# Start-up of a fused convolution and two-layer kernel: 64x64 tiles in the first units, x parts paired by tokens, and a moved plan of slots

## The chip, the cores and the metric

The kernel runs on one core of a Trainium2 chip. The metric is the device time of one execution in microseconds (us). Before the change the median of three runs is 680.96 us (680.73 to 681.37).

## What is computed

x has 8 sequences of 4096 tokens with 192 features each. A causal convolution over 7 tokens is taken, with softmax weights that are shared by the 24 features of one of 8 heads; its output goes through two matrices (192 x 2048 and 2048 x 192) with a leaky ReLU between them. Cut to what matters:

```python
w = softmax(weight)                                  # 8 heads x 7 taps
x_pad = concatenate([zeros((B, 6, D)), x], axis=1)
conv = einsum('hk,bskhg->bshg', w, windows_of(x_pad))  # each token and its 6 predecessors
h = conv.reshape(B * S, 192) @ w_in                  # w_in 192 x 2048
out = maximum(0.01 * h, h) @ w_out                   # w_out 2048 x 192
```

## The kernel before

**Tiling.** A block is 512 tokens of two sequences (e = 0 and 1), which take the two halves of the 128 partitions: `xt` holds x transposed, features on the partitions, in three chunks of 64 features (c = 0, 1, 2). There are 32 blocks. The first two are cut in halves of 256 tokens, so the list `groups` begins with groups 0 to 3 of 256 tokens (T = 256) and goes on with whole blocks from group 4 (T = 512).

**The work of one group.** The convolution of a group gives `yt`. `mm1` (L488) makes one unit of the first product: 3 chunks by 2 sequences, into a PSUM tile `ph` of two buffers; ACT applies the leaky ReLU and writes `g` (L515). A group of 256 tokens has 8 units, u = 0 to 7, a whole block has 16. A step j is two units. The second product is cut into slots. In groups 1 to 4 a slot is two matmuls for 128 tokens each (`mm2_row_slot`, L533; tile `po`), from group 5 on it works on whole blocks (`mm2_slot`, L568; tile `acc2`, shown as `acc` in the profile).

**Row slots.** 16 pieces of 128 tokens make 8 pairs of 32 slots. A pair has two rounds of 16 slots; in the second round the two row tiles of the array change banks, and its first matmuls wait for a "seal" (L545 to L549, `seal_round`, L555). The seal of pair p is the copy `evac_o(2p - 1)` (L631) of the odd piece of the pair before, made to wait for the last matmul of round one. That copy is on ACT. The odd copy also releases the output DMA of its pair, which stands in SP's queue.

**Who does the convolution.** For groups 0 and 1 chunks 0 and 2 are matmuls against diagonal matrices (`pe_conv_jobs`, L244; L259 in the profile), the others are chains of 7 instructions on DVE (`conv_jobs`, L209; L222 and L228). In the loop the jobs of group i+1 (`ahead`) are given to DVE while group i runs. In group 0 the diagonal matmuls for group 1 are put between the units in three portions, `CUTS` (L53): 6 steps after u = 1, 5 after u = 3, 3 after u = 5, each of 4 matmuls.

**How x gets there.** The first two blocks are loaded in four parts of 256 tokens, q = 0 to 3 (`load_first`, L137). Parts 1 and 2 come through POOL's queue as rows (`x_rows`), are transposed by TensorE (`transpose_first`, L162; part 1 inside unit 0 between chunks 1 and 2, part 2 after unit 6) and are copied from PSUM to `xt` by DVE (`evac_first`, L190). Part 3 and the later blocks are transposed by DMAs on SP's queue (L199, L114).

**Weights.** `w_in` comes in two halves n = 0, 1 of 1024 columns. Each is loaded for one half of the partitions and copied to the other by `spread_down` (L321) and `spread_up` (L324), mostly on DVE, with `near` and `far` for the two halves of its columns.

**Array tiles.** A matmul's tile of the array follows from its operands: the diagonal matmuls are 64x64, `mm1` in groups 0 to 4 uses weights of 128 columns (64x128), from group 5 on 64x64; the row slots are 64x128 and the transposes of `x_rows` 128x64.

**What sets the order.** Engines work in program order, and the order is written by hand: `plan` (L650) gives the slots of each step in groups 2, 3 and 4, `between` (L656) says in which steps some of them are put before the units of that step. DVE's queue in group i holds, step by step, the jobs of the next group's convolution.

Of the kernel before, what the change touches and what calls it, by code (L numbers as in the profile page):

```python
# [11 lines left out]
BF16 = mybir.dt.bfloat16  # L12
# [3 lines left out]
def kernel(  # L16
# [8 lines left out]
    nc = tc.nc  # L25
# [10 lines left out]
    CH = 64  # L36
    NCH = D // CH
    ST = 512
    SUB = ST // 128
    HT = ST // 2  # L40
    HS = SUB // 2
# [3 lines left out]
    NHALF = 2  # L45
# [4 lines left out]
    for k in range(K):  # L50
        SKEW += [(2, k), next(pair)]
    SKEW += [(1, 5), (0, 6), (1, 6)]
    CUTS = {1: (0, 6), 3: (6, 11), 5: (11, 14)}  # L53
    GB = 32
    NR = D // (2 * GB)

# [8 lines left out]
    psum_o = ctx.enter_context(tc.tile_pool(name="po", bufs=4, space=bass.MemoryType.PSUM))  # L65
# [70 lines left out]

    def load_first(q):  # L137
        rows = x[0:2, q * HT : (q + 1) * HT, :].rearrange("e (s p) d -> p e s d", s=HS)
        if q == 0:
            x_nat[q] = stage_pool.tile([128, 2, HS, D], FP32, name="x_nat")  # L140
            for s in range(HS):
                nc.sync.dma_start(out=x_nat[q][:, :, s], in_=rows[:, :, s])
        elif q in x_rows:
            for e in range(2):
                nc.gpsimd.dma_start(out=x_rows[q][:, e], in_=rows[:, e])  # L145
        else:
            for c in range(NCH):
                for e in range(2):
                    nc.gpsimd.dma_start(  # L149
                        out=x_half[q][:, c, :, e, :],  # L150
                        in_=rows[:, e, :, c * CH : (c + 1) * CH],
                    )
# [7 lines left out]
    ptr = {}  # L160

    def transpose_first(q, mid=None):  # L162
        if q:
            t = psum_o.tile([128, HS, NCH, 128], BF16, name="ptr", tag="po")
            for s, c in product(range(HS), range(NCH)):
                for e in range(2):
                    nc.tensor.transpose(  # L167
                        out=t[e * CH : (e + 1) * CH, s, c, :],
                        in_=x_rows[q][:, e, s, c * CH : (c + 1) * CH],
                        identity=ident,  # L170
                    )
            ptr[q] = [t[:, s] for s in range(HS)]
            return
        ts = [
            psum_o.tile([128, NCH, 128], FP32, name=f"ptr{s}", tag="po") for s in range(HS)
        ]
        for s, t in enumerate(ts):
            if s and mid is not None:
                mid()
            for c in range(NCH):  # L180
                nc.tensor.matmul(
                    out=t[:, c, :],
                    lhsT=x_half[q][:, c, s, :, :].rearrange("p e k -> p (e k)"),
                    rhs=ident,
                    start=True,
                    stop=True,
                )
        ptr[q] = ts

    def evac_first(q, *copies):  # L190
        dst = xt[0][:, :, HALO + q * HT : HALO + (q + 1) * HT]
        dst = dst.rearrange("p c (s k) -> p s c k", s=HS)
        for s, t in enumerate(ptr.pop(q)):
            for cs in (slice(0, 1), slice(1, NCH)) if q == 0 and s else (slice(0, NCH),):
                copies[s](out=dst[:, s, cs], in_=t[:, cs])

    def transpose_half(q):
# [82 lines left out]
    def run(*lists):  # L280
        for slots in zip_longest(*lists, fillvalue=()):
            for both in slots:
                for job in both:
                    job()
# [36 lines left out]
    def spread_down(n, copy=nc.vector.tensor_copy, cols=slice(0, WF)):  # L321
        copy(out=w_in[n][0:CH, 1, cols], in_=w_in[n][CH:128, 0, cols])  # L322

    def spread_up(n, slots=slice(0, 3, 2), cols=slice(0, WF)):  # L324
        to = slice(slots.start // 2 + 1, (slots.stop - 1) // 2 + 2)
        nc.vector.tensor_copy(out=w_in[n][CH:128, to, cols], in_=w_in[n][0:CH, slots, cols])  # L326
# [153 lines left out]
    NSW = 2 * NHALF  # L480
# [150 lines left out]
    def evac_o(n):  # L631
        b, e, s = subs[n]
        rp, st = divmod(b, NB)
        if n % 2 == 0 or n >= LAST:
            osb[n] = o_pool.tile([128, 2, D], FP32, name="o_sb")
        o_sb = osb[n if n >= LAST else n - n % 2]
        copy = nc.scalar.copy if b < NHALF else nc.vector.tensor_copy
        ins = copy(out=o_sb[:, n % 2, :], in_=po.pop(n))  # L638
        if n >= LAST:
            t0 = st * ST + s * 128  # L640
            nc.sync.dma_start(out=out_rows[2 * rp + e, t0 : t0 + 128, :], in_=o_sb[:, n % 2, :])
        elif n % 2 == 1:
# [7 lines left out]
    plan = {  # L650
        0: [0] * 4,
        NSW - 2: [16, 8, 8, 16],
        NSW - 1: [8, 8, 16, 16],
        NSW: [16, 8, 8, 16, 8, 8, 16, 16],
    }
    between = {(1, 0): (3, 5)}  # L656
    for i, js in ((NSW - 2, (2, 3)), (NSW - 1, (1, 2)), (NSW, (2, 3, 5, 6))):
        between.update({(i, j): (0, 4) for j in js})
    slot = 0

    def mm2_slots(i, n):
        nonlocal slot
# [7 lines left out]
    for i, grp in enumerate(groups):  # L670
        blk, t0, T = grp
        steps = T // 64
        if t0 == 0:
            g[blk] = g_pool.tile([128, NFC, 2, ST], BF16, name="g", tag="g")
        quota = plan.get(i, [16] * 4 if T == HT else [5, 5, 6, 5, 5, 6, 8, 8])
# [6 lines left out]
        for j in range(steps):  # L682
            early = between.get((i, j), (0, 0))
            for u in range(2 * j, 2 * j + 2):
                mm2_slots(i, early[u % 2])
                mm1(grp, u, 128 if i <= NSW else CH)
                if i == 0 and u == 0:
                    evac_first(1, nc.vector.tensor_copy, nc.vector.tensor_copy)
                    spread_up(0, slice(2, 3), far)
                    conv_1 = conv_jobs(groups[1], (1,))  # L690
                    run([conv_1[:3]])
                    spread_down(1)
                    spread_up(1, slice(0, 1), near)
                    spread_up(1, slice(2, 3))
                    run([conv_1[3:5]])
                    spread_up(1, slice(0, 1), far)
                    run([conv_1[5:]])
                    pe_0, evac_0 = pe_conv_jobs(groups[1], 0)
                    pe_2, evac_2 = pe_conv_jobs(groups[1], 2, cross=True)
                if i == 0 and u in CUTS:  # L700
                    cut = slice(*CUTS[u])
                    run(pe_0[cut], pe_2[cut])
                if i == 0 and u == 5:
                    evac_0(nc.vector.tensor_scalar_mul)
                    evac_2(nc.vector.tensor_scalar_mul, nc.vector.tensor_scalar_mul)
                if i == 0 and u == 6:
                    transpose_first(2)
                    evac_first(2, nc.vector.tensor_copy, nc.vector.tensor_copy)
            jobs = ahead[per * j : per * (j + 1)]
            if T == ST:  # L710

# [56 lines left out]
```

## Time and profile before

| | before |
|---|---|
| median of 3 runs | 680.96 us (680.73 to 681.37) |
| span of the profiled execution | 679.2 us |
| TensorE matmul (PE) | 674.9 us, 99%, 12442 matmuls |
| TensorE weight load (PEld) | 446.3 us, 66% |
| VectorE (DVE) | 481.2 us, 71% |
| ScalarE (ACT) | 517.6 us, 76% |
| GpSimd (POOL) | 147.4 us, 22% |
| DVE in 17.30 to 46.20 us | 10.46 of 10.50, 9.20 of 9.20, 9.15 of 9.20 us |
| POOL waiting for landed transposes | 405.6 us, 27 times |

A share is busy time over the span. PE's matmul times are pipelined and overlap, so a share of 99% says that the array always had a matmul in flight, not that it ran at its peak. In a timeline row the first number is the start, the second the length of the merged row, then engine, line, operation, tile written and tiles read, shapes and count; square brackets give the idle time in front and what ended it. In the chain of waits each row is a start, a length, an engine and a tile with its line; the chain is followed back from the last instruction. "64*128" is the tile of the array in rows and columns.

### The profile page before, as it was taken

To read this page: it belongs to the slowest core of one execution; us is meant where nothing else is said; L and a number is where in the kernel's file an instruction comes from. 1 tells how busy PE (TensorE), PEld (TensorE's weight loads), DVE (VectorE), ACT (ScalarE), POOL (GpSimd) and SP (SyncE) were. 2 spreads that over 40 slices of the span, in tenths; PEclk is the share of its full clock that TensorE was granted. 3 is DMA by queue.
4 is the path that set the end of the run, shared out by engine and by line. 5 is a ranking of instruction groups with operands and counts; after the bars stand their busy time and mean duration, and the time that the engine had idled before them with its cause. 6 is when DMAs were issued, how large, how long until landed. Compare 5 with 4: busy or idle time off the path is not lost.

```text
span 679.2 us, 27092 instructions
## 1 busy us (share of the span) xinstructions
PE 674.9 (99%) x12442; PEld 446.3 (66%) x12442; DVE 481.2 (71%) x816; ACT 517.6 (76%) x601; POOL 147.4 (22%) x208
## 2 busy tenths in 40 slices
PE   9999999999999999999999999999999999999998
PEld 6997666666666666666666666666666666666667
DVE  7989477866768766778667687667786676876612
ACT  7899877777787777777777777778777777777781
POOL 8455221122211222211222112222022220000000
PEclk9999999999999999999999999999999999999999
DMA  9999755655737656556556566567365573321123
GB/s 149 99 119 104 52 85 83 84 64 67 96 74 93 76 54 86 84 85 86 66 63 92 80 92 78 56 83 94 73 87 69 60 96 71 72 56 33 34 49 94
DMA packets 213970, 53.27 MB, mean 78 GB/s; under 512 B 209312, under 2 KB 213536, under 8 KB 213856
## 3 DMA queue, kind: packets, MB, share of 16 engines
q0 software_dynamic: 98832, 13.97, 30.3%
q1 hardware_dynamic: 115008, 37.57, 28.0%
q8 instruction: 97, 1.59, 0.9%
q14 instruction: 17, 0.14, 0.1%
q10 hardware_dynamic: 16, 0.00, 0.0%
HBM read 28.31 MB, written 25.17 MB: 79 GB/s over the span
## 4 chain that ended last, share of the span: by engine, by line
PE 98%; DVE 1%; ACT 0%; issue 0%; ACTq 0%
PE ph L507 49%; PE acc L588 44%; PE po L525 5%; PE acc L259 0%; DVE diag L420 0%; PE ptr L167 0%; ACT L366 0%; ACTq L288 0%; DVE w_in L322 0%; DVE yt L465 0%; DVE o_sb L638 0%; DVE x_half L155 0%; ACT w L372 0%; DVE w_in L326 0%; ACT junk L366 0%
## 5 line engine op out<-in xcount | busy, mean ns | idle before, releaser
L515 ACT ACTIVATE g<-ph 128x1024 bf16<-128x1024 f32 x512 | 496.6, 1021 | 139.8 <-PE ph L507 139.6
L228 DVE SCALAR_TENSOR_TENSOR yt<-xt,wk,yt 128x512 bf16<-128x512 bf16 (+1 forms) x582 | 380.1, 715 | 0.2
L507 PE MATMUL ph<-yt,w_in 64*64 64x512 bf16 (+2 forms) x6048 | 377.5, 369 | 0.3 <-DVE yt L465 0.3
L588 PE MATMUL acc<-g,w_out 64*64 64x512 bf16 x5568 | 339.9, 376 | 0.0
L507 PEld LDWEIGHTS <-w_in 64*64 64x64 bf16 (+1 forms) x6048 | 229.7, 131 | 103.4 <-issue 1.1
L588 PEld LDWEIGHTS <-w_out 64*64 64x64 bf16 x5568 | 178.2, 118 | 118.8
L96 POOL DMA_DIRECT2D x_bf<-in_x_dram x180 | 133.9, 774 | 407.6 <-DMA xt<-x_bf 405.6
L610 DVE STREAM_TRANSPOSE o_t<-acc 128x512 f32<-128x512 f32 x87 | 72.9, 875 | 182.2 <-PE acc L588 182.2
L525 PE MATMUL po<-w_out,g 64*128 64x192 bf16 (+1 forms) x640 | 36.8, 243 | 0.0
L525 PEld LDWEIGHTS <-g 64*128 64x128 bf16 (+1 forms) x640 | 32.6, 95 | 3.2 <-issue 0.4
L222 DVE TENSOR_SCALAR yt<-xt,wk 128x512 bf16<-128x512 bf16 (+1 forms) x97 | 28.8, 320 | 2.4 <-DMA xt<-x_bf 2.4
L598 ACT COPY junk<-junk 128x1 f32<-128x1 f32 x58 | 11.1, 191 | 4.1
L638 DVE COPY o_sb<-po 128x192 f32<-128x192 f32 x8 | 2.8, 356 | 6.8 <-PE po L525 3.9
L638 ACT COPY o_sb<-po 128x192 f32<-128x192 f32 x16 | 5.1, 323 | 0.3
L259 PE MATMUL acc<-xt,diag 64*64 64x256 bf16 x126 | 4.7, 272 | 0.1
L149 POOL DMA_DIRECT2D x_half<-in_x_dram x6 | 4.3, 732 | 0.9 <-DMA w_in<-in_moe_w_in_dram 0.9
L259 PEld LDWEIGHTS <-diag 64*64 64x64 bf16 x140 | 3.7, 106 | 1.0 <-issue 0.4
L360 PE MATMUL warm<-const-bfloat16-1.0 128*128 128x512 bf16 (+2 forms) x8 | 3.3, 577 | 0.8 <-PEq L752 0.8
L145 POOL DMA_DIRECT2D x_rows<-in_x_dram x4 | 2.9, 746 | 0.0
L316 POOL DMA_DIRECT2D w_in<-in_moe_w_in_dram x5 | 2.9, 593 | 0.0
L360 PEld LDWEIGHTS <-const-bfloat16-1.0 128*128 128x128 bf16 x10 | 1.2, 128 | 2.2 <-issue 2.2
L326 DVE COPY w_in<-w_in 64x512 bf16<-64x512 bf16 (+1 forms) x7 | 2.3, 337 | 0.2
(52 smaller groups left out, 25.9 us busy)
## 6 DMA issues: line engine op xcount, KB each, us to landing
out_dram<-o_t SPq DMA_DIRECT2D x112, 192.0 KB, 4.7
x_bf<-in_x_dram POOLq DMA_DIRECT2D x180, 64.0 KB, 3.1
out_dram<-o_sb SPq DMA_DIRECT2D x8, 192.0 KB, 2.8
xt<-x_bf SPq DMA_TRANSPOSE x90, 3.2
w_out<-in_moe_w_out_dram POOLq DMA_DIRECT2D x2, 384.0 KB, 8.3
out_dram<-o_t SPq DMA_DIRECT2D x8, 96.0 KB, 2.4
out_dram<-o_sb SPq DMA_DIRECT2D x8, 96.0 KB, 1.7
w_in<-in_moe_w_in_dram POOLq DMA_DIRECT2D x2, 256.0 KB, 5.5
```

The costliest lines, as they stand in the source:

```text
L96: ins = nc.gpsimd.dma_start(out=t[:, c, :, e, :], in_=src[2 * rp + e, :, :, c * CH : (c + 1) * CH],)
L222: lambda s=src, d=dst, c=c: nc.vector.tensor_scalar_mul(d, s, wk[:, c, 0:1])
L228: lambda s=src, d=dst, c=c, k=k: nc.vector.scalar_tensor_tensor(out=d, in0=s, scalar=wk[:, c, k : k + 1], in1=d, op0=mybir.AluOpType.mult, ...
L259: lambda k=k, p=p, a=a, ps=ps, to=to, acc=accs[e]: nc.tensor.matmul(out=acc[to, :T], lhsT=diag[c][ps, p, k, :], rhs=xt[0][ps, c, a : a + T ...
L360: nc.tensor.matmul(out=to[:, 0:cols], lhsT=ones[:, 0:128], rhs=ones[:, 0:cols], start=True, stop=True,)
L507: nc.tensor.matmul(out=ph[m : m + M, e, i * T : (i + 1) * T], lhsT=w_in_of(f, e, c, m, m + M), rhs=y[ps, c, t0 : t0 + T], start=(c == chun ...
L515: act = nc.scalar.activation(out=g[blk][:, nf * u : nf * (u + 1), :, t0 : t0 + T], in_=ph.rearrange("p e (i t) -> p i e t", i=nf), func=my ...
L525: return nc.tensor.matmul(out=po[m], lhsT=g[b][ps, fc, e, s * 128 : (s + 1) * 128], rhs=w_out[ps, fc, :], start=start, stop=stop,)
L588: ins = nc.tensor.matmul(out=acc2[gi, r][e * CH : (e + 1) * CH, 0:T], lhsT=w_out_of(ps, fc, r), rhs=g[b][ps, fc, e, t0 : t0 + T], start=fi ...
L598: seal = nc.scalar.copy(out=junk, in_=junk)
L610: nc.vector.transpose(out=osb[gi, 0][:, 0 : T // GB, :, r], in_=acc2.pop((gi, r))[:, 0:T].rearrange("p (j k) -> p j k", k=GB),)
L638: ins = copy(out=o_sb[:, n % 2, :], in_=po.pop(n))
```

## The change

Parts 1 and 2 of x are loaded with two neighbouring tokens on a partition, where before a partition held tokens p and p + 128. For part 1 the 12 transposes of 128x64 become 24 of 64x64 into two PSUM tiles, each with half of the tokens; both parts' copies to `xt` now take the tokens in pairs, and part 2's copies go by chunk (three of 256 elements, before two of 384). Units 0 and 1 of group 0 use weights of 64 columns, so twice the matmuls. The portions of the diagonal matmuls become 5, 5 and 4 steps after u = 1, 3 and 4; what followed u = 5 on DVE follows u = 4, with the last convolution job between the two evacuations. `spread_up(1, near)` moves ahead of `spread_down(1)`. In `plan`, group 3 has 56 slots in place of 48 and group 4 has 88 in place of 96, with more of them between units in group 4 and none in group 3. In group 4 the odd copies `evac_o` are on DVE; four copies leave ACT's list.

```diff
-    CUTS = {1: (0, 6), 3: (6, 11), 5: (11, 14)}
+    CUTS = {1: (0, 5), 3: (5, 10), 4: (10, 14)}
...
     def load_first(q):
         rows = x[0:2, q * HT : (q + 1) * HT, :].rearrange("e (s p) d -> p e s d", s=HS)
+        if q in x_rows:
+            rows = x[0:2, q * HT : (q + 1) * HT, :].rearrange("e (p s) d -> p e s d", s=HS)
...
     def transpose_first(q, mid=None):
+        if q == 1:
+            ts = [
+                psum_o.tile([128, HS, NCH, CH], BF16, name=f"ptr{r}", tag="po")
+                for r in range(2)
+            ]
+            for s, c in product(range(HS), range(NCH)):
+                for r, e in product(range(2), range(2)):
+                    ps = slice(r * CH, (r + 1) * CH)
+                    nc.tensor.transpose(
+                        out=ts[r][e * CH : (e + 1) * CH, s, c, :],
+                        in_=x_rows[q][ps, e, s, c * CH : (c + 1) * CH],
+                        identity=ident[ps, ps],
+                    )
+            ptr[q] = ts
+            return
         if q:
...
-            ptr[q] = [t[:, s] for s in range(HS)]
+            ptr[q] = t
             return
...
     def evac_first(q, *copies):
         dst = xt[0][:, :, HALO + q * HT : HALO + (q + 1) * HT]
+        if q == 1:
+            for r, t in enumerate(ptr.pop(q)):
+                half = dst[:, :, r * 128 : (r + 1) * 128]
+                copies[r](
+                    out=half.rearrange("p c (k s) -> p c k s", s=HS),
+                    in_=t.rearrange("p s c k -> p c k s"),
+                )
+            return
+        if q:
+            dst = dst.rearrange("p c (k s) -> p c k s", s=HS)
+            t = ptr.pop(q).rearrange("p s c k -> p c k s")
+            for copy, c in zip(copies, range(NCH)):
+                copy(out=dst[:, c], in_=t[:, c])
+            return
         dst = dst.rearrange("p c (s k) -> p s c k", s=HS)
...
+        split = turn == NSW and n % 2
-        copy = nc.scalar.copy if b < NHALF else nc.vector.tensor_copy
+        copy = nc.scalar.copy if b < NHALF and not split else nc.vector.tensor_copy
...
         NSW - 2: [16, 8, 8, 16],
-        NSW - 1: [8, 8, 16, 16],
-        NSW: [16, 8, 8, 16, 8, 8, 16, 16],
+        NSW - 1: [16, 16, 16, 8],
+        NSW: [8, 16, 8, 8, 16, 8, 8, 16],
     }
     between = {(1, 0): (3, 5)}
-    for i, js in ((NSW - 2, (2, 3)), (NSW - 1, (1, 2)), (NSW, (2, 3, 5, 6))):
+    for i, js in ((NSW - 2, (2, 3)), (NSW, (0, 1, 3, 4, 6, 7))):
         between.update({(i, j): (0, 4) for j in js})
...
-                mm1(grp, u, 128 if i <= NSW else CH)
+                mm1(grp, u, 128 if i <= NSW and (i, u) not in ((0, 0), (0, 1)) else CH)
                 if i == 0 and u == 0:
                     evac_first(1, nc.vector.tensor_copy, nc.vector.tensor_copy)
                     spread_up(0, slice(2, 3), far)
                     conv_1 = conv_jobs(groups[1], (1,))
                     run([conv_1[:3]])
+                    spread_up(1, slice(0, 1), near)
                     spread_down(1)
-                    spread_up(1, slice(0, 1), near)
                     spread_up(1, slice(2, 3))
                     run([conv_1[3:5]])
                     spread_up(1, slice(0, 1), far)
-                    run([conv_1[5:]])
+                    run([conv_1[5:6]])
...
-                if i == 0 and u == 5:
+                if i == 0 and u == 4:
                     evac_0(nc.vector.tensor_scalar_mul)
+                    run([conv_1[6:]])
                     evac_2(nc.vector.tensor_scalar_mul, nc.vector.tensor_scalar_mul)
                 if i == 0 and u == 6:
                     transpose_first(2)
-                    evac_first(2, nc.vector.tensor_copy, nc.vector.tensor_copy)
+                    evac_first(2, nc.vector.tensor_copy, nc.vector.tensor_copy, nc.vector.tensor_copy)
```

More of the change, by code (lines that the diff above doesn't have):

```diff
@@ L191, in evac_first @@
         dst = xt[0][:, :, HALO + q * HT : HALO + (q + 1) * HT]
+        if q == 1:
[12 more added lines that the diff above has]
+            return
         dst = dst.rearrange("p c (s k) -> p s c k", s=HS)
         for s, t in enumerate(ptr.pop(q)):
-            for cs in (slice(0, 1), slice(1, NCH)) if q == 0 and s else (slice(0, NCH),):
+            for cs in (slice(0, 1), slice(1, NCH)) if s else (slice(0, NCH),):
                 copies[s](out=dst[:, s, cs], in_=t[:, cs])
@@ L652 @@
         NSW - 2: [16, 8, 8, 16],
-        NSW - 1: [8, 8, 16, 16],
-        NSW: [16, 8, 8, 16, 8, 8, 16, 16],
+        NSW - 1: [16, 16, 16, 8],
+        NSW: [8, 16, 8, 8, 16, 8, 8, 16],
     }
     between = {(1, 0): (3, 5)}
-    for i, js in ((NSW - 2, (2, 3)), (NSW - 1, (1, 2)), (NSW, (2, 3, 5, 6))):
+    for i, js in ((NSW - 2, (2, 3)), (NSW, (0, 1, 3, 4, 6, 7))):
         between.update({(i, j): (0, 4) for j in js})
-    slot = 0
+    slot = turn = 0
     def mm2_slots(i, n):
@@ L672 @@
         steps = T // 64
+        turn = i
         if t0 == 0:
```

## The prediction

> **What bounds the kernel.** I read the page first: busy shares, then the chain that ended last.
>
> ```profile
> PE 674.9 (99%) x12442; PEld 446.3 (66%) x12442; DVE 481.2 (71%) x816; ACT 517.6 (76%) x601; POOL 147.4 (22%) x208
> ...
> PE 98%; DVE 1%; ACT 0%; issue 0%; ACTq 0%
> ```
>
> TensorE (PE) sets the end, and from 64.5 us on nothing is changed. So the question is when PE leaves group 4. Next, the chain in order of time over group 0 (start, length, piece):
>
> ```profile
> 8.09 0.63 PE ph L507 x8
> 8.72 0.46 PE ptr L167 x12
> 9.18 1.00 PE ph L507 x16
> 10.18 0.78 PE acc L259 x24
> 10.96 1.44 PE ph L507 x24
> 12.40 0.67 PE acc L259 x20
> 13.07 1.68 PE ph L507 x24
> 14.75 0.45 PE acc L259 x12
> ...
> 15.21 0.85 PE ph L507 x12
> 16.05 0.46 PE ptr L167 x12
> 16.51 0.78 PE ph L507 x12
> 17.29 0.25 PE po L525 x6
> ...
> 19.92 1.31 PE ph L507 x24
> ```
>
> The last line is the clean price: two units (24 matmuls, 12 concurrent pairs) 1.31, so 0.655 a unit and 0.109 a step of concurrent matmuls of 256 columns. The same two units cost 1.44 behind the diagonal matmuls (L259), so each change of array tile costs 0.13; 24 diagonal matmuls in fours are 6 x 0.109 + 0.13 = 0.78, as shown. Twelve transposes are 0.46 - 0.13 = 0.33. Two pieces are longer than this sum. The 1.68 holds 0.13 + 1.31 + 0.24, the 0.85 holds 0.13 + 0.655 + 0.065. The timeline names the first:
>
> ```profile
> 9.22 0.62 DVE L195 COPY xt<-ptr 128x384 bf16<-128x384 bf16 x2
> 12.21 0.42 DVE L322 COPY w_in<-w_in 64x1024 bf16<-64x1024 bf16 x1 [0.61 <-DMA w_in<-in_moe_w_in_dram]
> 12.64 0.77 DVE L326 COPY w_in<-w_in 64x512 bf16<-64x512 bf16 x2
> 13.46 1.02 PEld L507 LDWEIGHTS <-w_in 64*128 64x128 bf16 x19 [0.21 <-DVE w_in L326]
> ```
>
> PE waits for `w_in` half 1, which DVE can spread only when its DMA has landed. The 0.065 is unit 6 waiting for ACT to free `ph`. In groups 1 to 4 the pieces follow at the clean price. But DVE has no slack up to 46.15:
>
> ```profile
> 35.48 10.67 DVE L228 SCALAR_TENSOR_TENSOR yt<-xt,wk,yt 128x512 bf16<-128x512 bf16 x16
> 44.45 4.46 SPq L114 DMA_TRANSPOSE xt<-x_bf  x3
> 46.04 1.46 PE L507 MATMUL ph<-yt,w_in 64*128 64x512 bf16 x12
> 47.82 0.35 DVE L222 TENSOR_SCALAR yt<-xt,wk 128x512 bf16<-128x512 bf16 x1 [1.67 <-DMA xt<-x_bf]
> ```
>
> The convolution for group 4 ends on DVE at 46.15, and PE begins group 4 at 46.21 in the chain. Then DVE waits until 47.82 for block 3's transposes.
>
> **Part 1: tiles in units 0 and 1.** A unit of 64x64 tiles has 24 matmuls in 6 fours at 0.109, again 0.655. With transposes and diagonal matmuls also 64x64, the changes into the transposes, out of them, and into the first portion go: 3 x 0.13 = -0.39. The change in front of unit 0 hid in the wait for `yt` (L465, 7.56 to 8.05), so it gains nothing. From unit 1 on, the old and new orders have as many changes. Transposes: 24 in 6 fours of 64 columns. No row has the form. If a four takes what a pair took, 0.33; if issue of 24 binds, 24 x 0.028 (0.33/12) = 0.66; if it goes by columns, half, 0.17. I take 0.33, the nearest row; at 0.17 nothing is won, because PE then waits longer for DVE (next part), and at 0.66 DVE's copies would start 0.2 later: +0.2.
>
> **Part 2: pairs of tokens on DVE.** The copies of L195 now read PSUM with a stride of 192 elements between the two tokens of a pair. Before, 384 contiguous bf16 take 353 ns (mean). The low bound is that price. For the high one, DVE's copies of fp32 from PSUM: 96 elements 247 ns (L409), 192 elements 356 ns (L638): 1.14 ns an element, so 384 would take 574 ns. [...] Two copies overlap by 0.08 as before: 0.574 + 0.49 = 1.06, from 9.22 to 10.29, in place of 9.85. The first diagonal matmuls need this `xt`. PE would be ready at 10.18 - 2 x 0.13 = 9.92, and starts about 0.05 after DVE, 10.34: a new wait of +0.42. Behind these copies DVE has the far spread of half 0 (till 10.7; unit 2 wants it after 11.1) and three convolution jobs (till 12.05).
>
> [...]
>
> Part 2 of x: three copies of 256, by the same line 429 ns each, 0.43 + 2 x 0.345 = 1.12 in place of 0.62: DVE +0.50.
>
> **Part 3: `w_in` half 1.** The two x loads in front of it on POOL's queue have rows of two tokens: 256 packets in place of 512. In the first 22 us this queue's 5801 packets took 94.3% of 16 engines, 57 ns each. 256 x 57 / 16 = 0.9 us sooner at most, nothing if bytes bind; I take 0.45, a landing at 11.75. POOL's issues themselves are not on the path. DVE is free at 12.05, so the three spreads, 1.20 as before, end at 13.25. PE ends portion 2 at 12.98 (below) and wants the last spread two steps into unit 4, at 12.98 + 0.13 + 0.22 = 13.33. The wait goes: -0.24. If the landing stays, the spreads end at 13.41 and 0.13 of the wait remains. The swap of near and down changes nothing, as both come first.
>
> **Part 4: portions.** 5 + 5 + 4 steps are still 14. With the last portion between units 4 and 5, ACT (0.97 a unit) has the gap where it needed it: -0.065. PE from 10.34: portion 0.545 (10.89), two units 1.44 (12.33), portion 0.67 (13.0), unit 4 0.785, portion 0.57, two units 1.44, transposes 0.46, unit 7 0.785, so 17.03; before, 17.29. On DVE: two jobs and the far spread till 14.6, a job, evacuation of chunk 0 till 15.6, the job, chunk 2's till 17.1. Group 1's first unit wants chunk 2 at 17.03 + 0.25 + 0.22 = 17.5. Cover 0.4; if DVE ran later than that, its excess would be paid.
>
> **Part 5: plan and seals.** Eight slots, 16 matmuls in 8 pairs, are 8 x 0.082 = 0.66 of PE's work (1.32 for 32 matmuls in the chain) ahead of group 4's first unit, and as much less inside it: no net time. They buy cover: DVE starts the later convolutions 0.3 late (chunk 2 0.1 early, part 2's copies 0.50 late), so it ends that of group 4 at 46.4; PE comes there at 46.21 + 0.66 - 0.27 = 46.6. Without the moved slots this would cost 0.2 to 0.5.
>
> The seals of group 4 go from ACT to DVE, in order with the convolution of the next block, and only one unit (0.65) now stands between a round's last matmul and the first that waits. A copy is 0.356, with some 0.1 for the hand-over: 0.46, margin 0.19, if DVE is idle by then. First seal: DVE has two jobs in front, the second at 48.88 before. The transposes they wait for stand in SP's queue behind the output DMA of an ACT copy at the end of slot 143. In group 3 the new plan reaches that slot after 4 units and 32 slots, (37.01 - 0.27) + 2.62 + 2.64 = 42.0, not at 43.6; the transposes start at about 42.85, so the second job is at 47.3. The round ends at 46.6 + 2 x 0.65 + 0.66 = 48.55: DVE is waiting. Second: 8 jobs, some 5.0 us, from 48.95 to 54.0; the round ends at 55.1. Third: 8 x 0.667 from 55.5 to 60.8; ends at 61.6. Each time DVE is free first. Its idle time is late next for group 5: the last three jobs end at 64.05, PE wants them at 64.45. Cost: 0; if the transposes were not earlier, the first seal would cost 0.4. ACT loses four copies of 0.32 and gains no time for the end.
>
> **Sum.** -0.39 + 0.42 - 0.24 - 0.065 = -0.28 us. The profiled span 679.2 becomes 678.9; the median of the runs, 680.96, is 1.76 above the span, so 680.7. Own range of this case: DVE's copies and landing at their bounds, 680.3 to 681.1.
>
> **Rivals.**
> Seals stall PE (slower). Place: first matmul of the second round, three times. It decides as soon as DVE still has one L228 job (0.667) to do when the round ends: 0.667 + 0.46 - 0.65 = 0.48 each. The first alone: 680.7 + 0.4 = 681.1; all three: 682.1; in the middle 681.6. For it: DVE without slack up to 46.15 and in-order. Against: the free times above, 0.8 us or more.
> Paired copies cost nothing (faster). Then -0.42 more, but PE reaches unit 4 at 12.56 and the spreads end at 12.95 at the earliest, leaving 0.05 to 0.5 of the wait: 680.3 to 680.8. [...]
> The early landing does not come: 680.7 + 0.13 = 680.8, in the forecast's range; the straggling DMA (0.61 of DVE idle) speaks for it.
>
> **Numbers.** Forecast 0.5; seals 0.2; free copies 0.2; something that no row shows 0.1. 0.2% is 1.36 us, about what a measurement of this kernel can tell from no change. Faster needs 679.6: 0.04, from the last case and the tail of the third. Slower needs 682.3: 0.08, from the seals' tail and the last case. Same: 0.88. Range 680.0 to 681.9.
>
> **What will show it.** In the chain: no 0.13 at the transposes of unit 0; the first portion starting at 10.3 behind DVE's L195 copies at 0.57 each (0.35 would prove the rival); no `w_in` wait in unit 4; `po` starting at 17.0. On SP, block 3's transposes at 42.9. On PE no idle time behind an `o_sb` copy of DVE in 46 to 65 us. Any such wait, or groups 4 and 5 starting behind a convolution job, makes the forecast wrong.

## The result, and the profile after

The changed kernel takes 681.98 us (median of 21 runs, 681.23 to 682.93), the kernel before 680.96 (21 runs, 680.48 to 681.67). The ratio is 1.0016, 95% interval 1.0010 to 1.0021. The change costs 1.0 us.

The page of the profile after, first its span, then each engine's busy time, share of the span and number of instructions, then the shares of the chain of waits:

```profile
span 680.4 us, 27168 instructions
...
PE 675.4 (99%) x12478; PEld 447.0 (66%) x12478; DVE 484.4 (71%) x821; ACT 517.4 (76%) x597; POOL 146.8 (22%) x208
...
PE 99%; DVE 0%; issue 0%; ACT 0%
```

The span is 1.2 us longer, with 36 matmuls more. Shares do not show where; the stages do. Here each number is the time from one first matmul to another: of unit 0, of the first row slot (po), of group 5, and the last matmul. The column "before again" is a second profile of the unchanged kernel.

| stage, us | before | before again | after |
|---|---|---|---|
| span start to unit 0 | 8.09 | 8.09 | 8.25 |
| unit 0 to first row slot | 9.03 | 8.83 | 9.92 |
| first row slot to group 5 | 47.30 | 47.63 | 47.47 |
| group 5 to the end | 611.52 | 611.52 | 611.52 |

Nothing differs behind group 5. The loss is group 0: 0.89 of the 1.2. The start of unit 0 moves from run to run without any edit (7.89 in a second profile of after). The granted clock reaches full speed at 4.08 us in before and at 5.98 in after. That does not follow the edits strictly: it is 5.09 in experiment 7, which has group 0 as before, and 3.46 in experiment 9, which has it mostly as after. But the other nine profiles of after and its variants have it at 5.1 to 6.1, and the other four of before and its variants that record it at 3.5 to 4.1. Whether the edit has a part in this was not tried. What it can cost in group 0 is small: the first transposes start at 8.54 to 9.14 in the first family and at 8.59 to 9.06 in the second.

The chain of waits after, over group 0 (start, length, piece):

```profile
9.15 0.19 PE ptr L173 x15
...
9.44 1.01 DVE xt L212 x2
10.45 0.04 issue
10.50 0.74 PE acc L290 x20
11.24 1.43 PE ph L538 x24
12.67 0.87 issue
13.54 0.74 PE acc L290 x20
14.28 0.78 PE ph L538 x12
15.06 0.56 PE acc L290 x16
15.62 1.43 PE ph L538 x24
17.06 0.46 PE ptr L184 x12
...
17.52 0.85 PE ph L538 x12
18.37 0.25 PE po L556 x6
```

The piece that no step of the forecast has is the "issue" of 0.87: TensorE idles in front of the second portion of diagonal matmuls and nothing that the profile knows holds it. The portion's `xt` was there when DVE's copies ended at 10.45. The timeline of the same stretch shows that one weight load of the portion still ran, and the rest 0.84 later:

```profile
12.60 0.10 PEld L290 LDWEIGHTS <-diag 64*64 64x64 bf16 x1 [0.20 <-issue]
13.54 0.47 PEld L290 LDWEIGHTS <-diag 64*64 64x64 bf16 x19 [0.84 <-issue]
```

Around group 4, the timeline after of SP's queue (in brackets, where there are any, the idle time in front and what ended it) has block 3's transposes:

```profile
44.22 4.39 SPq L114 DMA_TRANSPOSE xt<-x_bf  x3
```

The timeline after of DVE has the two jobs that wait for them, and the first seal's copy:

```profile
47.34 0.35 DVE L253 TENSOR_SCALAR yt<-xt,wk 128x512 bf16<-128x512 bf16 x1 [0.48 <-PE ph L538]
49.09 0.35 DVE L253 TENSOR_SCALAR yt<-xt,wk 128x512 bf16<-128x512 bf16 x1 [1.40 <-DMA xt<-x_bf]
50.01 0.36 DVE L670 COPY o_sb<-po 128x192 f32<-128x192 f32 x1 [0.56 <-PE po L556]
```

The timeline after of the weight loads has the three places where a round waits for its seal:

```profile
50.42 0.30 PEld L556 LDWEIGHTS <-g 64*128 64x128 bf16 x8 [0.28 <-DVE o_sb L670]
57.00 0.28 PEld L556 LDWEIGHTS <-g 64*128 64x128 bf16 x8 [0.34 <-DVE o_sb L670]
63.56 0.28 PEld L556 LDWEIGHTS <-g 64*128 64x128 bf16 x8 [0.33 <-DVE o_sb L670]
```

DVE's second job (second row) starts at 49.09, 1.8 later than forecast. Behind it DVE stands idle for 0.56 until the round ends, and that is all the margin of the first seal's copy. The three seals hold back weight loads by 0.3, but the matmuls in front still cover all but 0.03 to 0.05 of each. So in this profile the seals look harmless. Experiments 3 and 4 have profiles in which they are not.

### The profile page after: what moved, and what is told of

Same layout as the page of the kernel before. It is cut to its first block, busy times and chain, and to the rows that moved or that the text cites. A ratio compares the mean times of both kernels' runs of the same rounds, so it can differ in the third digit from the quotient of the medians.

```text
span 680.4 us, 27168 instructions
## 1 busy us (share of the span) xinstructions
PE 675.4 (99%) x12478; PEld 447.0 (66%) x12478; DVE 484.4 (71%) x821; ACT 517.4 (76%) x597; POOL 146.8 (22%) x208
## 3 DMA queue, kind: packets, MB, share of 16 engines
q8 instruction: 97, 1.59, 0.9%
## 4 chain that ended last, share of the span: by engine, by line
PE 99%; DVE 0%; issue 0%; ACT 0%
PE ph L538 49%; PE acc L619 44%; PE po L556 5%; PE acc L290 1%; PE warm L391 0%; DVE xt L212 0%; PE ptr L198 0%; PE wps L391 0%; ACT yt L486 0%; PE ptr L184 0%; DVE o_sb L670 0%; PE ptr L173 0%; PE warm L427 0%; PE wps L427 0%; PE wps L290 0%
## 5 line engine op out<-in xcount | busy, mean ns | idle before, releaser
L259 DVE SCALAR_TENSOR_TENSOR yt<-xt,wk,yt 128x512 bf16<-128x512 bf16 (+1 forms) x582 | 381.7, 729 | 0.2
L538 PE MATMUL ph<-yt,w_in 64*64 64x512 bf16 (+3 forms) x6072 | 378.2, 369 | 0.1
L538 PEld LDWEIGHTS <-w_in 64*64 64x64 bf16 (+1 forms) x6072 | 230.5, 131 | 102.7 <-issue 1.1
L253 DVE TENSOR_SCALAR yt<-xt,wk 128x512 bf16<-128x512 bf16 (+1 forms) x97 | 30.3, 341 | 1.9 <-DMA xt<-x_bf 1.4
L629 ACT COPY junk<-junk 128x1 f32<-128x1 f32 x58 | 11.1, 192 | 4.1
L670 DVE COPY o_sb<-po 128x192 f32<-128x192 f32 x12 | 4.2, 357 | 9.6 <-PE po L556 4.9
```

The source lines that it names most:

```text
L253: lambda s=src, d=dst, c=c: nc.vector.tensor_scalar_mul(d, s, wk[:, c, 0:1])
L259: lambda s=src, d=dst, c=c, k=k: nc.vector.scalar_tensor_tensor(out=d, in0=s, scalar=wk[:, c, k : k + 1], in1=d, op0=mybir.AluOpType.mult, ...
L538: nc.tensor.matmul(out=ph[m : m + M, e, i * T : (i + 1) * T], lhsT=w_in_of(f, e, c, m, m + M), rhs=y[ps, c, t0 : t0 + T], start=(c == chun ...
L629: seal = nc.scalar.copy(out=junk, in_=junk)
```

## The experiments

They ran on several chips. Each median stands beside the kernel before on the same chip (680.8 to 681.2), so runs are compared by their ratios. "Issue" below means idle time like the 0.87.

**1. The same kernels once more.** One run each of after and before, without an edit.

> The changed kernel once more, for a second trace. Theory (instruction supply): in group 0 TensorE, with 64x64 tiles of 256 columns, goes through its instructions faster than they are fetched, and the 0.87 us of idle time in front of the second portion of diagonal matmuls comes back at the same instruction, between 0.3 and 1.5 us long; span 680.0 to 681.0. Rival (chance: one late fetch or a late clock in that run): no such idle time, span near 679.5.

> The kernel before once more, for a second trace. Supply theory: TensorE passes the same instruction (the 446th of its list) late enough that no idle time stands there; from unit 0 to the first row slot 9.0 to 9.1 us, span 679.0 to 679.6. Rival (the first trace of before was lucky): idle time without a named releaser in group 0, over 9.2.

After again: 681.45, span 679.7, unit 0 to row slot 9.66, with issue of 0.53 at the same instruction. Before again: 680.99, no issue. The idle time belongs to the changed kernel, and its length varies.

**2. More instructions ahead.** 36 short matmuls, four at a time, in place of two of the warm-up matmuls and of about their time: 34 more, each with a weight load.

```diff
-    warm(6, ST)
+    warm(4, ST)
     warm(1, 384)
+    for _ in range(9):
+        for r, e in product(range(2), range(2)):
+            ps = slice(r * CH, (r + 1) * CH)
+            nc.tensor.matmul(out=wa[e * CH : (e + 1) * CH, r, 0:112], lhsT=ones[ps, 0:CH],
+                             rhs=ones[ps, 0:112], start=True, stop=True)
```

> The changed kernel with two of the long warm-up matmuls replaced by 36 short ones of the same time, so that 34 more matmuls with their weight loads (68 instructions) stand in front of the same work. Supply: the idle place is a count of instructions, so it moves 68 instructions forward, into the first portion (after about 10 of its 20 matmuls), and is 0.5 to 1.7 us long; time 0 to 0.8 us above the changed kernel. Rival (a wait for data of the second portion, or for the array's tile change): the idle time stays in front of the second portion, 0.87 us.

682.71, ratio 1.0027 (1.0016 to 1.0039). Its chain of waits:

```profile
9.27 1.01 DVE xt L212 x2
10.29 0.04 issue
10.33 0.52 PE acc L290 x10
10.85 1.38 issue
12.23 0.52 PE acc L290 x10
```

The idle time has moved: it now cuts the first portion in two, and is longer. The two pauses differ in place by 34 matmuls, just as many as were put ahead. What counts is the number of the instruction, not the work.

**3. Fewer instructions.** Units 0 and 1 again with weights of 128 columns: 24 matmuls less.

```diff
-                mm1(grp, u, 128 if i <= NSW and (i, u) not in ((0, 0), (0, 1)) else CH)
+                mm1(grp, u, 128 if i <= NSW else CH)
```

> The changed kernel with units 0 and 1 back at weights of 128 columns: 48 instructions fewer in front of the second portion, two tile changes of 0.13 more. Supply: the idle time in front of the second portion goes (under 0.2 us left, further on), the time falls by 0.4 to 0.8 us below the changed kernel, to 681.2 to 681.6. Rival (the loss is DVE's strided copies and the seals): nothing falls, the two tile changes hide behind DVE's copies, 682.0.

No issue; unit 0 to row slot 9.24. 681.65, ratio 1.0009 (1.0000 to 1.0017): just above the range expected; some of the loss is back, not all. From the row slot to group 5 it takes 47.81, 0.34 more than after, and its weight load behind the first seal waits 0.64. Something new costs time once TensorE is earlier.

The traces tell what the pause waits for. In the record of DMA packets the instruction queue (97 packets of 16 KB in the whole span) moves its first one between 9.4 and 11.1 us. Set beside TensorE's 222nd and 223rd matmul, us from span start:

```
kernel                     first 16 KB packet   222nd   223rd   packet end to 223rd
before                      9.94 to 10.91       13.82   13.83   2.9
before again               10.80 to 11.84       13.58   13.77   1.93
after                      11.08 to 12.03       12.40   13.54   1.51
after again                10.67 to 11.64       12.12   12.92   1.28
more instructions (2)       9.95 to 10.90       10.58   12.23   1.33
fewer instructions (3)     11.08 to 12.03       13.56   13.67   1.64
tokens not paired (10)     10.47 to 11.43       11.99   12.77   1.34
old plan (5)               10.27 to 11.41       12.30   12.73   1.32
copies on ACT (8)          10.11 to 11.87       12.38   13.21   1.34
transposes earlier (13)    11.10 to 12.04       12.10   13.55   1.50
both out (14)              10.06 to 11.84       13.30   13.41   1.57
```

Wherever there is a pause, it lies between these two matmuls, and ends 1.3 to 1.5 after that packet. Where TensorE needs the 223rd later than that, there is none. So the pause, by these times, is TensorE waiting for its own instructions. The smaller tiles make 36 matmuls more of the same work, and bring the 223rd matmul from 13.8 forward to about 12.5, only 0.5 behind the end of the packet (12.03 in after).

The pause also has the size of the loss. Without one, the stretch that holds it (units 2 and 3, from their first matmul to the first of the second portion) takes 1.43. What it takes beyond that, in the six profiles with group 0 of the changed kernel (in experiment 2 the first portion, beyond its 0.67):

```
kernel                     unit 0 to row slot   lost in the pause   the rest
after                       9.92                0.94                8.98
after again                 9.66                0.60                9.06
more instructions (2)      10.64                1.68                8.96
old plan (5)                9.29                0.23                9.06
copies on ACT (8)           9.61                0.63                8.98
transposes earlier (13)    10.26                1.25                9.01
```

The five profiles with group 0 of the kernel before (before, before again, experiments 4, 6 and 7) take 9.03, 8.83, 8.87, 8.94 and 8.97. So the pause is nearly all that group 0 loses, and it differs from run to run with the time of the packet.

**4. The new plan and the copies on DVE, alone.** Before, with group 3 and 4's slots and the seals' copies of the changed kernel.

```diff
-        NSW - 1: [8, 8, 16, 16],
-        NSW: [16, 8, 8, 16, 8, 8, 16, 16],
+        NSW - 1: [16, 16, 16, 8],
+        NSW: [8, 16, 8, 8, 16, 8, 8, 16],
...
-    for i, js in ((NSW - 2, (2, 3)), (NSW - 1, (1, 2)), (NSW, (2, 3, 5, 6))):
+    for i, js in ((NSW - 2, (2, 3)), (NSW, (0, 1, 3, 4, 6, 7))):
...
-        copy = nc.scalar.copy if b < NHALF else nc.vector.tensor_copy
+        split = turn == NSW and n % 2
+        copy = nc.scalar.copy if b < NHALF and not split else nc.vector.tensor_copy
```

> The kernel before with only the new plan of slots and the four copies on DVE. Theory (seals): group 4 pays 0.05 us for each of three seals, and up to 0.4 more for the first where block 3's transposes land late; the rest of the plan costs nothing: 681.1 to 681.5. Rival (my prediction's cost of 0): 681.0. Rival (plan is a gain that group 0 hides): 680.6 or less.

682.25, ratio 1.0017 (1.0008 to 1.0026): as large a loss as the whole change, with group 0 untouched, and above the 681.1 to 681.5 expected. Its timeline of DVE:

```profile
49.58 0.62 DVE L222 TENSOR_SCALAR yt<-xt,wk 128x512 bf16<-128x512 bf16 x2 [3.07 <-DMA xt<-x_bf]
50.11 0.35 DVE L639 COPY o_sb<-po 128x192 f32<-128x192 f32 x1
```

And its timeline of TensorE at the first seal:

```profile
50.52 0.50 PE L525 MATMUL po<-w_out,g 64*128 64x192 bf16 x8 [1.16 <-DVE o_sb L639]
```

DVE stands 3.07 at a convolution job whose transposes have not landed, and the seal's copy is queued behind that job. TensorE idles 1.16. The first transposes were issued at 42.97, the second ones landed at 49.70, 6.7 later.

**5. The old plan in the changed kernel**, copies on ACT again (the edit above taken back).

> The changed kernel with the plan, the between-unit slots and the ACT copies of the kernel before. Theory (the seals on DVE cost 0.14 us in group 4 of the first trace, 0.03 to 0.05 each): 0.1 us less than the changed kernel from the seals, but the convolution of group 4 now ends on DVE 0.4 us after PE could begin it when PE is in time; as PE is 1 us late from group 0, nothing of that shows: 681.9. Rival (the plan and the seals are the loss): 681.0 or less.

681.62, ratio 1.0010 (1.0001 to 1.0019), 0.3 under the 681.9 expected; the pause happened to be short in its profile. The stall at the seal is out, but now group 4 starts behind DVE, whose last job for it ends at 46.96 (chain: "43.63 3.33 DVE yt L259 x5", then "47.00 1.27 PE ph L538 x10"), and from the row slot to group 5 it takes 47.82, 0.35 more than after. That is the cover which the moved slots were forecast to buy.

**6. The new plan with the copies on ACT.** Experiment 4 without its last two lines.

> Before with the new plan of slots, the odd copies of group 4 left on ACT. Theory (DVE's wait for block 3's transposes delays the first seal): no copy stands behind that wait, so the stall of 1.2 us at 50.5 goes; in its place a copy on ACT may stand behind one leaky ReLU (0.5 to 0.97), at most 0.3 at each of three seals. From po to group 5 47.3 to 48.0 (48.76 with the copies on DVE), median 681.1 to 681.7. Rival (the new plan itself costs the time, whoever copies): 48.7, 682.2.

682.94, ratio 1.0026 (1.0016 to 1.0035): the expectation (681.1 to 681.7) was wrong. From its chain of waits, one of three like rounds:

```profile
46.77 0.67 PE ph L507 x6
...
47.52 1.94 ACT g L515 x2
49.46 0.22 ACT o_sb L638
49.68 0.05 issue
49.73 0.50 PE po L525 x8
```

With one unit between a round's last matmul and the first that needs the seal, a copy on ACT stands behind two leaky ReLUs. Group 4 takes 19.30 in place of 18.38, a loss of 0.3 at each of three seals. So this run does not tell whether the plan or DVE's wait costs the time; it shows that the new plan needs the copies on DVE.

**7. Experiment 4, with the transposes earlier.** The x load of block 4 is issued behind block 3's transposes; the loads of blocks 4 and 5 (12 of 64 KB) stood ahead of them.

```diff
-            if j == steps // 4 and last_half and blk > 0:
+            if j == steps // 4 and last_half and blk > 0 and i != 3:
                 load_x(blk + 3)
             if j == steps // 2 and last_half and blk > 0:
-                transpose_x(blk + 2)
+                ins = transpose_x(blk + 2)
+                if i == 3:
+                    load_x(blk + 3, ins)
```

> Before with the new plan and the copies on DVE, and the x load of block 4 issued behind block 3's transposes. Theory (the transposes land late since x loads queued ahead of them fill the DMAs): the second transposes land 2.5 to 4.5 us after the first issue, at 45.5 to 47.5 (49.70 without the change), the first seal's copy ends by 49.7, its stall is under 0.3, po to group 5 47.4 to 47.9, median 681.1 to 681.5. Rival (something else holds the landing): it stays at 48.5 to 49.7 and the median at 682.0 to 682.3.

681.14, ratio 1.0006 (0.9997 to 1.0015): by the ratios 0.7 us under experiment 4, on another chip, and the two intervals overlap. Its timeline of DVE:

```profile
48.01 0.80 DVE L222 TENSOR_SCALAR yt<-xt,wk 128x512 bf16<-128x512 bf16 x2 [1.96 <-DMA xt<-x_bf]
48.85 0.36 DVE L639 COPY o_sb<-po 128x192 f32<-128x192 f32 x1
```

And of the weight load behind the first seal:

```profile
49.27 0.30 PEld L525 LDWEIGHTS <-g 64*128 64x128 bf16 x8 [0.28 <-DVE o_sb L639]
```

The copy runs 1.26 earlier and the stall is gone. The second transposes land at 48.43, 1.3 earlier and enough, though later than expected (45.5 to 47.5): from the first issue at 43.07 that is still 5.4 of the 6.7 us. So the loads ahead explain at most a part of the delay; what else holds the transposes was not tried. Nor does every profile with the loads ahead land as late as experiment 4's: the second transposes come at 48.40 to 49.98 in fourteen profiles with them, and at 48.09 to 48.74 in the three without (7, 13 and 14).

**8. After, with the copies on ACT.**

```diff
-        split = turn == NSW and n % 2
+        split = False
```

> After, with the odd copies of group 4 on ACT. Theory of two overlapping losses: the idle time at the 446th instruction (0.5 to 0.9) stays in group 0 and sets the time alone; u0 to po 9.6 to 9.9; median 681.5 to 681.9, little better than after. Rival (only the seals cost): 681.0 to 681.2.

**9. The same, with experiment 3's edit as well.**

> After, with weights of 128 columns in units 0 and 1 and the odd copies of group 4 on ACT: both suspected losses are out, all else of the change is kept. Theory: 681.0 to 681.4, from u0 to po 9.1 to 9.3 without idle time for issue, po to group 5 47.3 to 47.8. Rival (a third part of the change still costs): 681.6 or more.

683.28, ratio 1.0038 (1.0024 to 1.0052), and 683.00, 1.0031 (1.0019 to 1.0042). Both expectations missed for the reason of experiment 6: group 4 takes 19.3 with the new plan and copies on ACT. They say nothing of the two suspects, but experiment 9 has another wait, with no pause in front: in unit 4 a weight load stands 0.47 for DVE's spread of `w_in`.

**10. Tokens not paired.** After with the loads and copies of before (the transposes stay 64x64).

```diff
-        if q in x_rows:
-            rows = x[0:2, q * HT : (q + 1) * HT, :].rearrange("e (p s) d -> p e s d", s=HS)
...
-                half = dst[:, :, r * 128 : (r + 1) * 128]
-                copies[r](out=half.rearrange("p c (k s) -> p c k s", s=HS), in_=t.rearrange("p s c k -> p c k s"))
+                d4 = dst.rearrange("p c (s h k) -> p s c h k", s=HS, h=2)
+                copies[r](out=d4[:, :, :, r, :], in_=t)
...
-            dst = dst.rearrange("p c (k s) -> p c k s", s=HS)
-            t = ptr.pop(q).rearrange("p s c k -> p c k s")
-            for copy, c in zip(copies, range(NCH)):
-                copy(out=dst[:, c], in_=t[:, c])
+            dst = dst.rearrange("p c (s k) -> p s c k", s=HS)
+            t = ptr.pop(q)
+            for s in range(HS):
+                copies[s](out=dst[:, s], in_=t[:, s])
```

> The changed kernel without the pairing of tokens: the loads as before, the 64x64 transposes stay, the copies to xt read runs of 64 or more. Theory (supply): the copies take 0.35 each again and the first portion starts some 0.5 us sooner, but the next idle place ends when the instructions come, so it grows by as much and the w_in wait may come back: 681.8 to 682.2. Rival (the strided copies are the loss): 681.3 to 681.5.

681.64, ratio 1.0007 (0.9998 to 1.0016): the expectation (681.8 to 682.2) missed, by the ratios about half of the loss is back. The first portion starts at 10.03 without a wait for DVE, and issue of 0.51 stands at the second; from unit 0 to the row slot it takes 9.31. Part of what the fast copies win at the first portion (10.03 in place of 10.50) is waited away at the 223rd matmul.

**11. Pairing alone.** Before, with paired tokens and 128x64 transposes; two paired copies for each part.

```diff
+        if q in x_rows:
+            rows = x[0:2, q * HT : (q + 1) * HT, :].rearrange("e (p s) d -> p e s d", s=HS)
...
+        if q:
+            dst = dst.rearrange("p c (k s) -> p c k s", s=HS)
+            t = ptr.pop(q).rearrange("p s c k -> p c k s")
+            for r in range(2):
+                ks = slice(r * CH, (r + 1) * CH)
+                copies[r](out=dst[:, :, ks], in_=t[:, :, ks])
+            return
```

> Before, with only the pairing of tokens (part 1 transposed in tiles of 128x64 as before, two paired copies; part 2 the same way). Theory (the strided copies make VectorE and so group 0 longer): copies 0.55 to 0.6 each, the first portion starts 0.3 to 0.5 later, the wait for w_in in unit 4 stays or grows; u0 to po 9.2 to 9.6 (8.83 to 9.03 in four runs without it), median 681.2 to 681.6. Rival (slack takes it up): 8.8 to 9.1, 680.9 to 681.1.

681.52, ratio 1.0006 (0.9997 to 1.0015). The copies take 1.02 the two, unit 0 to row slot 9.17; by the profile a cost of some 0.1 to 0.3 is likely, but the interval holds no change.

**12. Portions and spreads alone.** Before with the new `CUTS`, the evacuations behind u = 4 and near before down.

```diff
-    CUTS = {1: (0, 6), 3: (6, 11), 5: (11, 14)}
+    CUTS = {1: (0, 5), 3: (5, 10), 4: (10, 14)}
...
-                    spread_down(1)
                     spread_up(1, slice(0, 1), near)
+                    spread_down(1)
...
-                    run([conv_1[5:]])
+                    run([conv_1[5:6]])
...
-                if i == 0 and u == 5:
+                if i == 0 and u == 4:
                     evac_0(nc.vector.tensor_scalar_mul)
+                    run([conv_1[6:]])
```

> The kernel before with only the portions after units 1, 3 and 4, the evacuations a unit sooner and the near spread ahead of the spread down. Theory: the 0.065 us wait of unit 6 for ACT goes and nothing else moves, the wait for w_in stays: 680.8 to 681.0. Rival (the sooner portion makes unit 5 wait or gives the w_in wait away): 680.5.

681.13, ratio 1.0000 (0.9991 to 1.0008). The wait for `w_in` is out of its chain ("13.47 0.78 PE ph L507 x12"), yet unit 0 to row slot is 9.15, no shorter than before. Two numbers of the traces explain that. Unit 0 takes 0.84 to its first transposes (0.56 in before), as ACT's piece of `yt` comes late in this profile; the edit touches nothing ahead of them. And there was little to win: from the first transposes to the row slot it takes 8.31, against 8.47 in before and 8.27 in before again.

**13. After, with the transposes earlier** (experiment 7's edit), and **14. the same with experiment 3's edit**: the second suspect alone taken out of the changed kernel, and both.

> After, with the x load of block 4 issued behind block 3's transposes. Theory: in the changed kernel TensorE comes a unit of time late from group 0 and so hides the first seal's wait; the gate takes away only the 0.1 that was left there. u0 to po 9.6 to 9.9 with idle time for issue, po to group 5 47.3 to 47.5, median 681.5 to 681.9. Rival (the late transposes are the loss in the changed kernel too): 680.9 to 681.2.

> After, with weights of 128 columns in units 0 and 1 and the x load of block 4 behind block 3's transposes: idle time for issue and late transposes are both out. Theory: po to group 5 47.3 to 47.5 in place of 47.81 without the gate; u0 to po 9.2 to 9.6, by VectorE's longer copies; median 681.2 to 681.6, 0.2 to 0.4 under the kernel without the gate (681.65). Rival (the two do not add): 681.65 or more.

Transposes earlier alone: 681.82, ratio 1.0014 (1.0005 to 1.0023). Group 0 keeps its issue (1.17 in this profile, 10.26 from unit 0 to the row slot, more than the 9.6 to 9.9 expected), and from there to group 5 it takes 47.47 as in after: nothing is won. Both out: 681.29, ratio 1.0004 (0.9995 to 1.0013). Its chain over the disputed place:

```profile
10.38 0.74 PE acc L290 x20
11.12 1.44 PE ph L538 x24
12.56 0.67 PE acc L290 x20
13.23 0.84 PE ph L538 x12
```

No idle time, 9.15 to the row slot, 47.47 to group 5. By the ratios, 0.0016 for the whole change, taking out the second loss alone gives back 0.0002 (13), the first alone 0.0007 (3), both together 0.0012: 0.1, 0.5 and 0.8 us. These intervals overlap, and experiments 5 and 10 alone give back about as much as 3 (0.0006 and 0.0009). The stages show why the two do not simply add. What decides at the first seal is how long behind the first row slot the second transposes land. Of the nine profiles with the new plan and the copies on DVE, seven have 30.5 to 31.4 us between the two, and take 47.43 to 47.49 from the row slot to group 5. Experiment 3 has 31.9 and takes 47.81, experiment 4 has 32.7 and takes 48.76. TensorE that waits 0.9 for instructions comes late to the row slot and so has next to nothing to wait for at the seal; without the first wait it can pay the second. But the landing has its own part: after again reaches the row slot at 17.55 as experiment 3 does, and is spared by a landing at 48.40 in place of 49.46. None of the versions is faster than before beyond its interval.

## Why the prediction was wrong

The forecast was 680.7 with no change likeliest; the result lies just above its range, at 681.98. Step by step:

- **The array tiles (part 1)** are the step that failed. The same work in 64x64 tiles of 256 columns is twice as many instructions. The step weighed 24 x 0.028 for the issue of the transposes, and put the supply of the list at nothing without a reason. The runs show a pause there: 0.87 in after, 0.53 in its second profile, 1.17 in experiment 13. The term of -0.39 was too large as well. Experiment 10 has these tiles and no wait in front of the first portion, and starts it at 9.91, before at 10.11, with unit 0 at 8.10 and 8.09: 0.20 is won, and nothing more in the portion itself. In after DVE's copies cover the difference.
- **Paired copies (part 2)** came as forecast: 1.01 for 1.06, and the first portion started at 10.50, that is 10.34 and the 0.16 by which unit 0 was later. The rival "paired copies cost nothing" fell. That a paired copy of 384 elements costs 574 ns was the author's estimate from fp32 copies of 96 and 192 elements, and no run shows that figure: in after the two take 546 and 557 ns, where the unpaired ones of before take 347 to 358, and the pair 1.01 against 0.62. Part 2's three paired copies of 256 elements take 414 to 425 ns, 1.09 for all, where 429 and 1.12 were forecast.
- **The sum over group 0** used pieces of the chain for places behind a wait, where they do not fit: the portion of 20 diagonal matmuls behind DVE's copies is a piece of 0.74, forecast 0.545. TensorE is not slower there: from the first matmul of a portion of 20 to the first of the next unit it takes 0.67 or 0.68, with a wait in front (both in after) and without one (the second in before, the first in experiment 10). In a running stream a piece begins at the end of the matmul before; behind a wait it begins with its own first matmul and holds all of that one's 0.27, where the forecast has a step of 0.109. That is most of the 0.19 at the first portion; at the second, with 0.67 forecast, it is 0.07.
- **`w_in` (part 3)**: the wait is not in after (unit 4 takes 0.78), but by luck: TensorE comes 0.87 late. DVE's spreads end at 13.64, not at 13.25. Without the pause unit 4 takes 0.95 in experiment 3 and 0.84 in 14, and stands 0.47 for `w_in` in experiment 9. The wait was not worth 0.24 either: from the first matmul of units 4 and 5 to the next portion it takes 1.67 in before, and 1.53 to 1.57 in before again and experiments 4, 6 and 7, where no weight load of theirs waits for `w_in`.
- **Portions (part 4)**: the 0.065 did not go, it is now in unit 7, whose piece is 0.85. With these, 0.87 + 0.19 + 0.07 + 0.07 = 1.20 over the forecast's 17.03 + 0.16, and the chain has po at 18.37, 1.18 later. Of this the pause is 0.94 (0.87 and the second 0.07). The other 0.24 is gain that did not come: the forecast took 0.28 off group 0, and even less the pause it takes 8.96 to 9.06 from unit 0 to the row slot, no less than before.
- **Plan and seals (part 5)**: "the transposes start at about 42.85, so the second job is at 47.3" failed. The issue was right: 42.97 where group 0 was not late. The landing does not follow the issue. In five profiles whose first transposes were issued at 42.97, 43.60, 43.60, 44.22 and 44.73, the second landed at 49.70, 48.40, 49.46, 49.07 and 49.18 (experiment 4, after again, experiment 3, after, experiment 5). The moved slots brought the issue forward, and with it the seal, but not the data that DVE waits for in front of the seal's copy. The rival "seals stall PE" had the place right. Its condition was that DVE still has an L228 job to do; DVE stood idle instead, for data. The step's own "if the transposes were not earlier, the first seal would cost 0.4" was 1.16 by experiment 4. In the changed kernel a late group 0, or an early landing, hides this.
- **Moved slots buy cover**: experiment 5 has group 4 behind DVE at 46.96 without them. This step stands.

Experiment 14 still lies 0.2 to 0.3 above before, which its interval does not tell from none. In its profile that lies in front of the first transposes (0.84 from unit 0, as in experiment 12); from there to the row slot it takes 8.31. Why ACT's piece of `yt` comes late in some profiles stays open.

## What to carry to other kernels

Count instructions as well as columns when tiles get smaller early in a kernel: here a pause called "issue" (0.87 us in after) stood behind the 222nd matmul even when 34 matmuls were put ahead of it, and was, by the times in experiment 3, the engine waiting for its own program. Before an evacuation is moved to another engine, look at what stands in front of it there and what that waits for; a transfer that is issued earlier has not landed earlier until a profile shows it (the transposes issued at 42.97 in experiment 4 landed at 49.70, those issued at 44.22 in after at 49.07). When two suspects give back little one at a time, take out both in one run before either is cleared.

## What the runs showed of the hardware

The instruction queue moves packets of 16 KB (1.59 MB in 97). That they hold TensorE's list is an estimate from their number: 97 for 12478 matmuls and as many weight loads would be 257 to a packet, some 64 bytes each. From the page of the profile after (queue, packets, MB, share of 16 engines):

```profile
q8 instruction: 97, 1.59, 0.9%
```

The first packet of this queue starts as late as 9.4 to 11.1 us, takes 0.95 to 1.8, and TensorE goes on 1.3 to 1.5 after its end. In all seven profiles with a pause it stopped after the 222nd matmul and the 223rd weight load. How the 445 instructions ahead of that place reached the engine no trace shows. Why the first packet comes at that time was not tried; the loads' own DMA traffic is heavy there (94.3% of 16 engines for their queue in the first 22 us of before).

The landing of a transpose by DMA varied more than any step allowed for: 2.43 us after its issue at 57.23 in experiment 6, 6.5 at 42.97 in experiment 4 behind 12 loads of x. The first of block 3 takes 2.4 to 6.5 in the fourteen profiles with these loads ahead, and 2.9 to 4.8 in experiments 7, 13 and 14 without them. In these three the first of block 4 takes 5.7 to 7.5, elsewhere 2.4 to 4.6: the delay may only have moved.
